# Gated linear attention and two feed-forward layers: attention products split into 64-column tiles

## The chip, the cores and the metric

One Trainium2 chip, one core. The metric is the device time of one execution in microseconds, the median of several runs. TensorE (PE in the profile) does the matrix products, VectorE (DVE), ScalarE (ACT) and GpSimd (POOL) the rest, and SyncE (SP) issues the DMAs. The stationary operand of a product is loaded into the array by an instruction of its own, LDWEIGHTS (PEld in the profile); the MATMUL then streams the other operand through. The array has 128 rows (the contraction) and 128 columns (the stationary operand's columns, which become the output's partitions).

## The reference

Three layers. First a gated linear attention, for 4 batch entries and 8 heads of 48, over 768 positions:

```python
f = 1.0 / (1.0 + np.exp(-f_logit))
for t in range(S):
    state = f[:, :, t, :, None] * state + np.einsum('bhd,bhe->bhde', k[:, :, t], v[:, :, t])
    y[:, :, t] = np.einsum('bhd,bhde->bhe', q[:, :, t], state)
```

The outputs of the 8 heads side by side are 3,072 rows of 384. Then a normalised, gated layer of width 1,536, `(silu(xn @ w_gate) * (xn @ w_val)) @ w_out` with `xn = x / rms * rms_g`, and a layer of width 2,048, `g(x @ w_in) @ w_out` with a piecewise quadratic `g`. All data are fp32.

## The kernel before, in words

The 768 positions are cut into 6 chunks of C = 128. A **unit** u is one chunk of one batch entry: 24 units, chunk n = u // 4, batch entry b = u % 4. `attention` (L382) does one unit for all 8 heads, which are taken in NP = 4 pairs p. A pair of heads lies on partitions 0 to 47 and 64 to 111 (HP = 64; PD = 112 rows in use), so that one product serves both heads or each head has one half of the rows. Inside a chunk the recurrence becomes products, with q and k scaled by running products of the gates (scans on VectorE, L419 to L430):

- `turned` (L433, products on L435) transposes k, 4 products.
- `scores` (L442, products on L446): for each p and each head i, the 128 x 128 matrix of k against q; k of 48 rows and 128 columns is stationary, q streams 128 columns. 8 products, alternating between rows 0 to 47 and 64 to 111. VectorE multiplies the two score tiles by the causal mask (L449), tile W (or sg).
- `update` (L454, products on L456): for each p, transposed k (112 columns) stationary, v of both heads (96 columns) streams. The result has the two 48 x 48 blocks wanted, one for each head, and two that belong to no head. 4 products. VectorE adds the wanted blocks to the state (L481, or L486 in the first chunk), so that the blocks that no head owns stay zero. The units of the last chunk leave this out.
- `read` (L466): for each p, q against the state of the pair (L471; 128 stationary columns, 96 streamed; not in the first chunk, where the state is zero), then for each head the masked scores against v (L473; 128 stationary columns, 48 streamed), all accumulated in tile y. 4 x (1 + 2) = 12 products.

Each of these fp32 products stands as two LDWEIGHTS and two MATMUL records in the trace. Then the row norm (L489 to L495), a transposition (`xpose`, L500, on L502), and a split into a high and a low part, xh and xl (L511, L513), for the next layer.

The feed-forward products are done in three parts of a narrower fp32 (`mm3`, L517, on L519 to L521): high by high, low by high, high by low, each 128 x 128 stationary and 512 streamed (the 4 batch entries of one chunk), one record each. For each chunk j, 12 steps of the first layer (gate, value, output) make 324 such products; after the 6 chunks the second layer follows, 6 x 16 steps. Weights are loaded and split into two parts once (`weights`, L349; L365 to L376 on ScalarE, VectorE and GpSimd), those of the first layer before and during the first chunk.

The order on every engine is made by a planner (`Plan`, L50) before the program runs: `add` gives it each operation with its engine, a cost in ns, a due position and, for TensorE, the streamed columns; it simulates the engines and emits the operation that can start first, by due position where several can. The units of chunk j + 1 are due spread over the projections of chunk j. Units 0 to 3 come before the first projection; there the planner fills TensorE's idle time with products that nothing reads (`keep_clock`, L571, on L574). PSUM tiles are few: two "a" (transposed k, scores, update, transposition), two "h" (projections), three "o", one "y".

Of the kernel before, what the change touches and what calls it, by code (L numbers as in the profile page):

```python
# [16 lines left out]
B, H, S, D = 4, 8, 768, 48  # L17
C = 128
NCH = S // C
NU = NCH * B  # L20
NP = H // 2
HP = 64
PD = HP + D
VD = 2 * D
# [25 lines left out]
class Plan:  # L50
# [28 lines left out]
    def add(self, eng, cost, pos, fn, r=(), w=(), new=(), after=(), cols=0, at=0.0, table=None, lock=False):  # L79
        i = len(self.ops)  # L80
        deps = set(after)
        for key in r:
            deps.update(self.writer.get(key, ()))
        for key in w:
            deps.update(self.writer.get(key, ()))
            deps.update(self.readers.get(key, ()))
        for tag, key in new:
            if tag != "a" and tag in self.last:
                self.turn.setdefault(i, []).append(self.last[tag])
            self.last[tag] = i  # L90
            self.maker[key] = i
        for key in (*r, *w):
            base = key[0] if isinstance(key, tuple) else key
            if base in self.maker:
                deps.add(self.maker[base])
        for key in w:
            self.writer[key] = (i,)
            self.readers[key] = []
        for key in r:
            self.readers.setdefault(key, []).append(i)  # L100
        deps.discard(i)
        where = {eng: cost} if isinstance(eng, str) else {}
        if not where:
            for e, c in eng.items():
                if isinstance(c, tuple):
                    self.away[i, e] = c[1]
                    c = c[0]
                where[e] = c
        self.ops.append([where, None, pos, fn, deps, tuple(new), set(k for k in (*r, *w)), not isinstance(eng, str), cols, at, table, lock])
        return i  # L110
# [140 lines left out]
def dve(n, fast=False):  # L251
    return (65 + (n / 2 if fast else n)) / 0.96
# [6 lines left out]
def pool(n):  # L259
    return 250 + 2.0 * n  # L260
# [20 lines left out]
def gla_moe_moe2_kernel(ctx, tc, q, k, f, v, w_in, w_out, rms_g, w2, ident, cmask, hmask, out):  # L281
    nc = tc.nc
    pl = Plan()
    pl.engines = {"DVE": nc.vector, "Pool": nc.gpsimd, "ACT": nc.scalar}
    T = pl.T
    add = pl.add
# [38 lines left out]
    st = [const.tile([PD, NP, VD], F32, name=f"st{b}") for b in range(B)]  # L325
# [54 lines left out]
    updated = []  # L380

    def attention(u, due, g):  # L382
        n, b = divmod(u, B)
        last = u + B >= NU
        early = u < B
        fk, Fk, kk, qk, vk, yk, xk = (f"{nm}{u}" for nm in ("f", "F", "k", "q", "v", "y", "xn"))
        guest = early and u >= 2
        if guest:
            g0 = f"e{u}"
            kk, qk, vk, fk = ((g0, nm) for nm in ("k", "q", "v", "f"))  # L390
            fk = ("e4", "f" if u == 2 else "g")

        def at(x):
            return due + (x - 11) * g

        def v4(key):
            return T[key][0:PD].rearrange("p (a b) -> p a b", a=NP)
# [4 lines left out]
        def rows(h):  # L402
            return slice(h * HP, h * HP + D)
# [3 lines left out]
        if early or u % 2 == 0:  # L407
            keys = [fk] if early else [f"f{u}", f"f{u + 1}"]
            for o, key in enumerate(keys):
# [4 lines left out]
                w=keys, table="sigmoid")  # L414
# [6 lines left out]
            r=[fk, "floor"], w=[Fk], new=[("F", Fk)], lock=True)  # L421
# [4 lines left out]
            r=["back"], w=[fk], lock=True)  # L426
# [4 lines left out]
        ktk, tpk, uk = f"kT{u}", f"tp{u}", f"U{u}"  # L431
        if not last:
            def turned():  # L433
# [4 lines left out]
                r=[tpk], w=[ktk], new=[("kT", ktk)])  # L438
        aks, wks = [f"a{u}_{i}" for i in range(2)], [f"W{u}_{i}" for i in range(2)]
        tags = [("h", "sg") if early and i else ("a", "W") for i in range(2)]  # L440

        def scores():  # L442
            kt, qt = v4(kk), v4(qk)
            for p in range(NP):
                for i in range(2):
                    nc.tensor.matmul(T[aks[i]][:, p * C:(p + 1) * C], lhsT=kt[rows(i), p], rhs=qt[rows(i), p], start=True, stop=True)  # L446
        scored = add("PE", 4 * 222, at(2), scores, cols=1536, r=[kk, qk], w=aks, new=[(tags[i][0], aks[i]) for i in range(2)])
        for i in range(2):
            add("DVE", dve(4 * C), at(2 + i), lambda ak=aks[i], wk=wks[i]: nc.vector.tensor_tensor(  # L449
                T[wk].rearrange("p (a b) -> p a b", a=4), T[ak].rearrange("p (a b) -> p a b", a=4),  # L450
                cm.rearrange("p (o a) -> p o a", o=1).to_broadcast([C, 4, C]), op=ALU.mult),
                r=[aks[i], "cm"], w=[wks[i]], new=[(tags[i][1], wks[i])])
        if not last:
            def update():  # L454
                for p in range(NP):
                    nc.tensor.matmul(T[uk][0:PD, p * VD:(p + 1) * VD], lhsT=T[ktk][:, p * PD:(p + 1) * PD],  # L456
                                     rhs=T[vk][:, p * VD:(p + 1) * VD], start=True, stop=True)
            updated.append(add("PE", 4 * 196, at(5), update, cols=4 * 384, r=[ktk, vk], w=[uk], new=[("a", uk)], after=[scored]))

        def block(h):  # L460

            return st[b][rows(h), :, h * D:(h + 1) * D]
# [3 lines left out]
        def read():  # L466
            y, vt = T[yk], T[vk]
            for p in range(NP):
                c0 = p * VD
                if n:  # L470
                    nc.tensor.matmul(y[:, c0:c0 + VD], lhsT=v4(qk)[:, p], rhs=st[b][:, p], start=True, stop=False)  # L471
                for h in range(2):
                    nc.tensor.matmul(y[:, c0 + h * D:c0 + (h + 1) * D], lhsT=T[wks[h]][:, p * C:(p + 1) * C],  # L473
                                     rhs=vt[:, c0 + h * D:c0 + (h + 1) * D], start=(n == 0), stop=(n == 0 or h == 1))
        add("PE", 4 * (444 + (224 if n else 0)), at(6), read, cols=4 * (384 + (384 if n else 0)),
            r=[*wks, vk, qk, *(sks if n else [])], w=[yk], new=[(ytag, yk)])
        if not last:
            for h in range(2):
                uu = lambda h=h: T[uk][rows(h), 0:NP * VD].rearrange("p (a b) -> p a b", a=NP)[:, :, h * D:(h + 1) * D]
                if n:  # L480
                    add("DVE", dve(NP * D), at(8), lambda h=h, uu=uu: nc.vector.tensor_tensor(  # L481
                        block(h), block(h), uu(), op=ALU.add), r=[uk], w=[sks[h]])
                    add({"Pool": pool(NP * D), "DVE": dve(NP * D)}, 0, at(18), lambda eng, h=h: eng.tensor_tensor(
                        block(h), block(h), ends_of[rows(h)].to_broadcast([D, NP, D]), op=ALU.mult), r=[("fca", u)], w=[sks[h]], lock=True)
                else:
                    add("DVE", dve(NP * D), at(18), lambda h=h, uu=uu: nc.vector.tensor_tensor(  # L486
                        block(h), uu(), ends_of[rows(h)].to_broadcast([D, NP, D]), op=ALU.mult), r=[uk, ("fca", u), "zero"], w=[sks[h]])
# [4 lines left out]
            r=[ssk], w=[msk], new=[("ms", msk)])  # L492
        add("Pool", 520, at(8), lambda: nc.gpsimd.tensor_tensor(T[rik], T[msk], mhalf, op=ALU.pow),
            r=[msk, "halves"], w=[rik], new=[("ri", rik)])
# [14 lines left out]
        def tv():  # L509
            return T[tk][:, 0:DM].rearrange("p (a b) -> p a b", a=KD)  # L510
        add("ACT", act(DM, True), at(11), lambda: nc.scalar.copy(halves_of(xh), tv()),  # L511
            r=[tk], w=[(xh, o)], new=[("xh", xh)] if o == 0 else [])
        return add("DVE", dve(DM), at(11), lambda: nc.vector.tensor_tensor(  # L513
            halves_of(xl), tv(), halves_of(xh).bitcast(F32), op=ALU.subtract),
            r=[tk, (xh, o)], w=[(xl, o)], new=[("xl", xl)] if o == 0 else [])
# [73 lines left out]
    for u in range(B):  # L589
        attention(u, due0[u], 0.7)  # L590
# [9 lines left out]
    for j in range(NCH):  # L600
        step = SEG * (base[j + 1] - base[j]) / long
        if j + 1 < NCH:
            for o in range(B):
                done = attention(B * (j + 1) + o, base[j + 1] - 3.0 - (B - 1 - o) * (long + FILL) / B * 0.95, 2.0)
        oks = [f"o{e}_{j}" for e in range(KD)]
        xk = (f"xh{j}", f"xl{j}")
        for i in range(F1):
            p0 = base[j] + 3 * i * step
            gk, vk = f"hg{j}_{i}", f"hv{j}_{i}"
            sk = f"sg{j}_{i}"  # L610
            seg_in(gk, wk1[i][0], xk, range(B), p0)
            add("ACT", act(TB, True), p0 + step, lambda sk=sk, gk=gk: nc.scalar.activation(  # L612
                T[sk], T[gk], AF.Silu), r=[gk], w=[sk], new=[("sg", sk)], table="silu")
            seg_in(vk, wk1[i][1], xk, range(B), p0 + step)
            add("DVE", dve(TB), p0 + 2 * step, lambda sk=sk, vk=vk: nc.vector.tensor_tensor(  # L615
                T[sk], T[sk], T[vk], op=ALU.mult), r=[vk], w=[sk])
            phk, plk = split_p(sk, p0 + 2 * step)
            seg_out(oks, wk1[i][2], phk, plk, p0 + 5 * step, i == 0, i == F1 - 1)
        evac(oks, [x1d[j][:, e] for e in range(KD)], [("x1d", j, e) for e in range(KD)],
             base[j] + 3 * F1 * step + 3 * step, ["ev", "F", "ev"])  # L620
# [4 lines left out]
    for j in range(NCH):  # L625
        b0 = base2 + 2 * F2 * SEG * j
        xk = (f"xh2_{j}", f"xl2_{j}")
        for e, tg in enumerate(("f", "q", "f")):
            rk = f"x1r{j}_{e}"
            load(lambda rk=rk: T[rk][:, 0:TB], x1d[j][:, e], 128 * 2048, b0 - 44 + 4 * e, rk, [(tg, rk)],  # L630
                 r=[(("x1d", j, e), 0)], after=[done])
            add("ACT", act(512), b0 - 24 + 4 * e, lambda rk=rk, e=e, xk=xk: nc.scalar.copy(T[xk[0]][:, e], T[rk][:, 0:TB]),
                r=[rk], w=[(xk[0], 10 + e)], new=[("xh", xk[0])] if e == 0 else [])
            add("DVE", dve(512), b0 - 24 + 4 * e, lambda rk=rk, e=e, xk=xk: nc.vector.tensor_tensor(
                T[xk[1]][:, e], T[rk][:, 0:TB], T[xk[0]][:, e].bitcast(F32), op=ALU.subtract),
                r=[rk, (xk[0], 10 + e)], w=[(xk[1], 10 + e)], new=[("xl", xk[1])] if e == 0 else [], lock=True)
# [18 lines left out]
    def count():  # L655
# [5 lines left out]
        r=["mn", "hm"], w=["cnt"], new=[("a", "cnt")])  # L661
# [185 lines left out]
```

## Time and profile before

| | |
|---|---|
| median of 3 runs | 998.58 us (998.14 to 999.08) |
| the profiled execution's own time | 997.97 us |
| its span, from the first to the last instruction | 996.2 us |
| mean granted TensorE clock in it | 0.997 of full |
| busy: TensorE, VectorE, ScalarE, GpSimd | 983.0, 583.2, 357.3, 78.4 us |
| matmul records | 5064 |

How to read it: busy times are of one profiled execution. Matmuls overlap each other, and their ends are modelled; a record's duration is longer than its distance from the next one, so the cost of a group is read from the distance between starts. A busy share is a mean over stages with different limits; the table of stretches parts them.

### The profile page before, as it was taken

The numbers are of one execution on the slowest core, as the hardware profiler recorded it, in microseconds if no ns is written. First come the engines' busy times: TensorE is split into PE (matmuls) and PEld (weight loads), VectorE is DVE, ScalarE is ACT, GpSimd is POOL, SyncE is SP. The second block draws the span as 40 slices with busy tenths as digits, with TensorE's granted clock in tenths as the row PEclk, the third lists the DMA queues.
The fourth block names the chain that finished last, engine by engine and source line by source line (L and its number), as shares of the span: only waits on it lengthen the run. The fifth ranks groups of instructions, "written<-read, shape, count | busy, mean of one in ns | idle before, by whom it ended". The sixth has DMA issues, their size and how long they took to land.

```text
span 996.2 us, 12717 instructions
## 1 busy us (share of the span) xinstructions
PE 983.0 (99%) x5064; PEld 820.5 (82%) x5064; DVE 583.2 (59%) x886; ACT 357.3 (36%) x590; POOL 78.4 (8%) x82
## 2 busy tenths in 40 slices
PE   8999999999999999999999999999999999999997
PEld 7888888888888888888888888888888888888885
DVE  6998966335633563365336997555565555655544
ACT  3465623322432242223224555333343333333332
POOL 2404121001000110011000100000000000000000
PEclk9999999999999999999999999999999999999999
DMA  9971112101211121011005541010010010100001
GB/s 279 340 244 38 38 50 70 36 29 58 67 28 45 48 70 36 29 62 56 22 1 190 189 159 64 1 64 1 0 64 1 22 43 1 64 1 0 32 1 35
DMA packets 26500, 64.22 MB, mean 64 GB/s; under 512 B 3136, under 2 KB 6848, under 8 KB 26432
## 3 DMA queue, kind: packets, MB, share of 16 engines
q1 hardware_dynamic: 26432, 63.32, 19.8%
q8 instruction: 42, 0.69, 0.3%
q14 instruction: 26, 0.21, 0.1%
HBM read 53.87 MB, written 9.44 MB: 64 GB/s over the span
## 4 chain that ended last, share of the span: by engine, by line


## 5 line engine op out<-in xcount | busy, mean ns | idle before, releaser
L519 PE MATMUL h<-xh,w 128*128 128x512 f32 x720 | 284.2, 395 | 0.0
L521 PE MATMUL h<-xh,w 128*128 128x512 f32 x720 | 280.7, 390 | 0.0
L520 PE MATMUL h<-xl,w 128*128 128x512 f32 x720 | 280.2, 389 | 0.0
L519 PE MATMUL o<-ph,w 128*128 128x512 f32 x504 | 199.1, 395 | 0.0
L520 PE MATMUL o<-pl,w 128*128 128x512 f32 x504 | 196.6, 390 | 0.0
L521 PE MATMUL o<-ph,w 128*128 128x512 f32 x504 | 196.6, 390 | 0.0
L521 PEld LDWEIGHTS h<-xh,w 128*128 128x128 f32 x720 | 135.1, 188 | 28.8
L519 PEld LDWEIGHTS h<-xh,w 128*128 128x128 f32 x720 | 135.2, 188 | 27.9
L520 PEld LDWEIGHTS h<-xl,w 128*128 128x128 f32 x720 | 135.3, 188 | 27.1
L646 DVE SCALAR_TENSOR_TENSOR k<-sg,h 128x512 f32<-128x512 f32 x96 | 66.1, 688 | 97.8 <-ACT sg L644 97.2
L615 DVE TENSOR_TENSOR sg<-sg,h 128x512 f32<-128x512 f32 x72 | 49.2, 683 | 123.3 <-PE h L521 122.5
L520 PEld LDWEIGHTS o<-pl,w 128*128 128x128 f32 x504 | 94.7, 188 | 20.1 <-DVE pl L556 1.3
L519 PEld LDWEIGHTS o<-ph,w 128*128 128x128 f32 x504 | 94.7, 188 | 19.9
L521 PEld LDWEIGHTS o<-ph,w 128*128 128x128 f32 x504 | 94.6, 188 | 19.8
L555 ACT CAST ph<-k 128x512 fp32r<-128x512 f32 x96 | 59.5, 619 | 132.3 <-DVE k L648 132.3
L644 ACT ACTIVATE sg<-h,halves 128x512 f32<-128x512 f32 x96 | 66.1, 688 | 113.4 <-PE h L521 113.4
L556 DVE TENSOR_TENSOR pl<-k,ph 128x512 fp32r<-128x512 f32 x96 | 66.5, 692 | 64.6 <-ACT ph L555 64.6
L612 ACT ACTIVATE sg<-h 128x512 f32<-128x512 f32 x72 | 43.0, 597 | 116.6 <-PE h L521 116.5
L555 ACT CAST ph<-sg 128x512 fp32r<-128x512 f32 x72 | 44.6, 620 | 109.7 <-DVE sg L615 109.7
L648 DVE SCALAR_TENSOR_TENSOR k<-sg,k 128x512 f32<-128x512 f32 x96 | 66.5, 692 | 3.0
L556 DVE TENSOR_TENSOR pl<-sg,ph 128x512 fp32r<-128x512 f32 x72 | 51.9, 721 | 21.3 <-ACT ph L555 21.0
L473 PE MATMUL y<-v,W 128*128 128x48 f32 x328 | 47.1, 265 | 0.0
(114 smaller groups left out, 851.2 us busy)
## 6 DMA issues: line engine op xcount, KB each, us to landing
w<-in_w SPq DMA_DIRECT2D x16, 768.0 KB, 4.5
w<-in_w_in SPq DMA_DIRECT2D x12, 768.0 KB, 11.8
k<-in_k SPq DMA_DIRECT2D x22, 256.0 KB, 2.8
f<-in_f SPq DMA_DIRECT2D x22, 226.6 KB, 2.7
q<-in_q SPq DMA_DIRECT2D x22, 224.0 KB, 2.8
w<-in_w_out SPq DMA_DIRECT2D x6, 768.0 KB, 11.9
v<-in_v SPq DMA_DIRECT2D x22, 192.0 KB, 2.8
x1d<-ev SPq DMA_DIRECT2D x12, 256.0 KB, 2.0
```

Of the source, the lines that this page charges most:

```text
L473: nc.tensor.matmul(y[:, c0 + h * D:c0 + (h + 1) * D], lhsT=T[wks[h]][:, p * C:(p + 1) * C], rhs=vt[:, c0 + h * D:c0 + (h + 1) * D], start= ...
L519: nc.tensor.matmul(o, lhsT=wh, rhs=xh, start=start, stop=False)
L520: nc.tensor.matmul(o, lhsT=wh, rhs=xl, start=False, stop=False)
L521: nc.tensor.matmul(o, lhsT=wl, rhs=xh, start=False, stop=stop)
L555: add("ACT", act(TB), pos, lambda: nc.scalar.copy(T[phk], T[pk]), r=[pk], w=[phk], new=[("ph", phk)])
L556: add("DVE", dve(TB), pos, lambda: nc.vector.tensor_tensor(T[plk], T[pk], T[phk].bitcast(F32), op=ALU.subtract), r=[pk, phk], w=[plk], new ...
L612: add("ACT", act(TB, True), p0 + step, lambda sk=sk, gk=gk: nc.scalar.activation(T[sk], T[gk], AF.Silu), r=[gk], w=[sk], new=[("sg", sk)], ...
L615: add("DVE", dve(TB), p0 + 2 * step, lambda sk=sk, vk=vk: nc.vector.tensor_tensor(T[sk], T[sk], T[vk], op=ALU.mult), r=[vk], w=[sk])
L644: add("ACT", act(512, True, 1), p0 + SEG, lambda ak=ak, hk=hk: nc.scalar.activation(T[ak], T[hk], AF.Relu, bias=half, scale=0.5), r=[hk, " ...
L646: add("DVE", dve(512), p0 + SEG, lambda ak=ak, gk=gk, hk=hk: nc.vector.scalar_tensor_tensor(T[gk], T[ak], 1.0, T[hk], op0=ALU.min, op1=ALU ...
L648: add("DVE", dve(512), p0 + SEG, lambda ak=ak, gk=gk: nc.vector.scalar_tensor_tensor(T[gk], T[ak], 1.0, T[gk], op0=ALU.min, op1=ALU.mult), ...
```

## The change

Three of the four groups of products are cut in two. In `scores` and `read` the stationary operand's 128 columns become two products of 64, whose outputs are partitions 0 to 63 and 64 to 127 of the same tile; each half streams what the whole did. In `update` each pair's product becomes two, one for each head: 48 stationary columns, 48 streamed, the output on partitions 0 to 47 and 64 to 111; the blocks that belong to no head are not computed, and the result lies 48 instead of 96 columns apart. The costs and columns that the planner is told are changed with them.

```diff
         def scores():
             kt, qt = v4(kk), v4(qk)
             for p in range(NP):
-                for i in range(2):
-                    nc.tensor.matmul(T[aks[i]][:, p * C:(p + 1) * C], lhsT=kt[rows(i), p], rhs=qt[rows(i), p], start=True, stop=True)
-        scored = add("PE", 4 * 222, at(2), scores, cols=1536, r=[kk, qk], w=aks, new=[(tags[i][0], aks[i]) for i in range(2)])
+                for x in range(2):
+                    for i in range(2):
+                        nc.tensor.matmul(T[aks[i]][x * HP:(x + 1) * HP, p * C:(p + 1) * C], lhsT=kt[rows(i), p, x * HP:(x + 1) * HP],
+                                         rhs=qt[rows(i), p], start=True, stop=True)
+        scored = add("PE", 600, at(2), scores, cols=1200, r=[kk, qk], w=aks, new=[(tags[i][0], aks[i]) for i in range(2)])
...
             def update():
                 for p in range(NP):
-                    nc.tensor.matmul(T[uk][0:PD, p * VD:(p + 1) * VD], lhsT=T[ktk][:, p * PD:(p + 1) * PD],
-                                     rhs=T[vk][:, p * VD:(p + 1) * VD], start=True, stop=True)
-            updated.append(add("PE", 4 * 196, at(5), update, cols=4 * 384, r=[ktk, vk], w=[uk], new=[("a", uk)], after=[scored]))
+                    for h in range(2):
+                        nc.tensor.matmul(T[uk][rows(h), p * D:(p + 1) * D], lhsT=T[ktk][:, p * PD + h * HP:p * PD + h * HP + D],
+                                         rhs=T[vk][:, p * VD + h * D:p * VD + (h + 1) * D], start=True, stop=True)
+            updated.append(add("PE", 550, at(5), update, cols=1200, r=[ktk, vk], w=[uk], new=[("a", uk)], after=[scored]))
...
             for p in range(NP):
                 c0 = p * VD
-                if n:
-                    nc.tensor.matmul(y[:, c0:c0 + VD], lhsT=v4(qk)[:, p], rhs=st[b][:, p], start=True, stop=False)
+                for x in range(2 if n else 0):
+                    nc.tensor.matmul(y[x * HP:(x + 1) * HP, c0:c0 + VD], lhsT=v4(qk)[:, p, x * HP:(x + 1) * HP], rhs=st[b][:, p],
+                                     start=True, stop=False)
                 for h in range(2):
-                    nc.tensor.matmul(y[:, c0 + h * D:c0 + (h + 1) * D], lhsT=T[wks[h]][:, p * C:(p + 1) * C],
-                                     rhs=vt[:, c0 + h * D:c0 + (h + 1) * D], start=(n == 0), stop=(n == 0 or h == 1))
-        add("PE", 4 * (444 + (224 if n else 0)), at(6), read, cols=4 * (384 + (384 if n else 0)),
+                    for x in range(2):
+                        nc.tensor.matmul(y[x * HP:(x + 1) * HP, c0 + h * D:c0 + (h + 1) * D],
+                                         lhsT=T[wks[h]][:, p * C + x * HP:p * C + (x + 1) * HP],
+                                         rhs=vt[:, c0 + h * D:c0 + (h + 1) * D], start=(n == 0), stop=(n == 0 or h == 1))
+        add("PE", 4 * (230 + (170 if n else 0)) + 150, at(6), read, cols=4 * (384 + (384 if n else 0)),
             r=[*wks, vk, qk, *(sks if n else [])], w=[yk], new=[(ytag, yk)])
         if not last:
             for h in range(2):
-                uu = lambda h=h: T[uk][rows(h), 0:NP * VD].rearrange("p (a b) -> p a b", a=NP)[:, :, h * D:(h + 1) * D]
+                uu = lambda h=h: T[uk][rows(h), 0:NP * D].rearrange("p (a b) -> p a b", a=NP)
```

## Rows read from the trace of the kernel before

**Rows 1.** The page: busy times, the slices of TensorE, the costliest groups (two of six).

```profile
PE 983.0 (99%) x5064; PEld 820.5 (82%) x5064; DVE 583.2 (59%) x886; ACT 357.3 (36%) x590; POOL 78.4 (8%) x82
...
PE   8999999999999999999999999999999999999997
...
L519 PE MATMUL h<-xh,w 128*128 128x512 f32 x720 | 284.2, 395 | 0.0
...
L519 PE MATMUL o<-ph,w 128*128 128x512 f32 x504 | 199.1, 395 | 0.0
```

**Rows 2.** Timeline of TensorE among projections; start us, us, engine, line, what.

```profile
301.21 0.39 PE L519 MATMUL h<-xh,w 128*128 128x512 f32 x1
...
303.25 0.39 PE L519 MATMUL h<-xh,w 128*128 128x512 f32 x1
```

**Rows 3.** Table of stretches: length; PE, PEld, DVE, ACT, POOL busy; PEclk; DMA share; GB/s.

```profile
25.00:45.18 20.18, 19.79 (x194) 17.66 (x195) 18.86 (x33) 8.32 (x21) 10.65 (x8) 1.00 1.03 335
45.18:135.88 90.70, 90.50 (x509) 76.33 (x507) 83.46 (x119) 53.25 (x80) 22.77 (x19) 1.00 0.34 111
142.00:239.00 97.00, 96.63 (x547) 81.44 (x546) 45.69 (x76) 28.38 (x52) 8.68 (x11) 1.00 0.16 47
520.00:990.00 470.00, 469.08 (x2068) 386.88 (x2066) 283.93 (x412) 178.18 (x274) 2.57 (x1) 1.00 0.14 48
```

**Rows 4.** TensorE's waits, longest total first; total us, times, longest.

```profile
PE a L456 <- ACT kT L437: 2.0, 1, 2.0
```

**Rows 5.** TensorE's groups by line, 45.1 to 519 us: the read's.

```profile
L473 PE MATMUL y<-v,W 128*128 128x48 f32 x320 | 45.6, 265 | 0.0
L471 PE MATMUL y<-st,q 112*128 112x96 f32 x160 | 33.1, 288 | 0.0
```

**Rows 6.** Timeline of TensorE around one unit's scores.

```profile
309.68 0.39 PE L520 MATMUL h<-xl,w 128*128 128x512 f32 x1
309.91 0.39 PE L521 MATMUL h<-xh,w 128*128 128x512 f32 x1
310.23 1.16 PE L446 MATMUL a<-q,k 48*128 48x128 f32 x16
311.32 0.50 PE L519 MATMUL h<-xh,w 128*128 128x512 f32 x1
```

**Rows 7.** Timeline of TensorE: scores of a unit with score tiles a and h.

```profile
34.04 0.27 PE L446 MATMUL a<-w 48*128 48x128 f32 x1
34.05 0.27 PE L446 MATMUL h<-w 48*128 48x128 f32 x1
34.15 0.27 PE L446 MATMUL a<-w 48*128 48x128 f32 x1
```

**Rows 8.** Timeline of TensorE: an update, its read at once behind it.

```profile
317.58 0.93 PE L456 MATMUL a<-v,kT 128*112 128x96 f32 x8
318.34 0.39 PE L471 MATMUL y<-st,q 112*128 112x96 f32 x2
...
318.97 0.43 PE L471 MATMUL y<-st,q 112*128 112x96 f32 x2
...
319.64 0.43 PE L471 MATMUL y<-st,q 112*128 112x96 f32 x2
...
320.97 0.48 PE L519 MATMUL h<-xh,w 128*128 128x512 f32 x1
```

**Rows 9.** Timeline of TensorE's weight loads among projections.

```profile
309.68 0.19 PEld L521 LDWEIGHTS h<-xh,w 128*128 128x128 f32 x1
```

**Rows 10.** Timeline of TensorE: an update with projections behind it.

```profile
390.38 0.93 PE L456 MATMUL a<-v,kT 128*112 128x96 f32 x8
391.09 0.48 PE L519 MATMUL h<-xh,w 128*128 128x512 f32 x1
```

**Rows 11.** Timeline of TensorE before the first projection.

```profile
41.21 2.47 PE L574 MATMUL o<-spin 128*128 128x256 bf16 x21
...
43.84 1.58 PE L574 MATMUL o<-spin 128*128 128x256 bf16 x13
```

## The prediction

> **What bounds the kernel now.** I began with the page's busy shares and its slices: TensorE is busy 99% of the span, and in every slice but the first and the last [rows 1]. Matmul ends are modelled, so I checked this on start times. In the projections one 512-column matmul follows another every 2.04/9 = 0.227 us [rows 2], and the 3 x (720 + 504) = 3,672 of them [rows 1] make 834 us of the 996.2 us span. The table of stretches, read next, says what else is near its limit: TensorE is full in each of them. VectorE is busy 83.46 of 90.70 us while the first chunk's projections run, and only 45.69 of 97.00 us in a later chunk; from 520 us on, where no attention is left, the change can touch nothing [rows 3]. The list of TensorE's waits is short: the longest totals 2.0 us [rows 4]. So from 45 us to 518 us each microsecond taken off TensorE's own stream is a microsecond off the end, if VectorE keeps up.
>
> What TensorE spends on attention there: scores, update, and the read's two groups, the state's on L471 and the values' on L473. Each fp32 product makes two records: 20 units x 4 p x 2 heads are 160 products, and 320 records [rows 5]. For one unit (one batch entry, one chunk) the timeline gives:
>
> Scores, 16 records, take 311.32 - 310.23 = 1.09 us [rows 6]. In a unit whose two score tiles have different names (a and h) the records can be told apart: the two heads' records, on rows 0 to 47 and 64 to 111, start within 0.01 us of each other, and such a pair starts every 0.111 us [rows 7]. Two row halves thus run side by side. Eight pairs are 0.89 us; the other 0.20 us, and 0.09 us ahead of the block (0.32 us since the last projection record where 0.227 is usual), are what going into and out of this split costs: 0.29 us.
>
> The update takes 0.76 us (8 records of 112 stationary columns, 0.095 each) and the read 2.63 us (24 records) [rows 8]. One p of the read is 6 records in 0.67 us, 0.111 each, though two of them stream 96 columns and four only 48. What they share is a load of 128 stationary columns. So the load sets the pace: 0.111/128 = 0.87 ns a column, and the update's 0.095/112 = 0.85 agrees.
>
> **The change, part by part.** Every product is split into twice as many with 64 stationary columns (48 in the update), on alternate column halves. No row shows a column split. The question is whether the two halves' loads run side by side, as row halves do [rows 7], or in turn. Side by side, a pair costs 64 x 0.87 = 0.056 us where one record cost 0.111; in turn it costs 0.111 and nothing is won. These are the two ends. I take the first, as the row split is the nearest row: same loads, same instruction, a different half.
>
> The Trainium skill ("TensorE: Matmul & The Clock Gate", Part 3, What overlaps and what doesn't) has a rule against this: weight loads overlap with running matmuls only where the row group differs, and column halves share theirs. By it the loads go in turn (second rival). As a general rule this trace contradicts it: the load for L521 starts at 309.68, with the L520 matmul of the same 128 rows [rows 9, 6].
>
> Scores: 8 groups of four records instead of 8 pairs, 8 x 0.056 = 0.45, and the same 0.20 around them: 0.65 against 1.09, saves 0.44. The split by rows was there already, so no new entry is paid. x20 units = 8.8 us.
>
> Update: 8 pairs of 48 columns, 8 x 48 x 0.87 ns = 0.34 against 0.76, saves 0.42. The last chunk has none: x16 = 6.7 us. That the diagonal blocks alone are made also halves the streamed columns, worth nothing by itself, since the load sets the pace.
>
> Read: 24 pairs, 24 x 0.056 = 1.34 against 2.63, saves 1.29; x20 = 25.8 us.
>
> New entries and exits: update and read had no split around them, and now each run of them pays the 0.29 us of the scores. In 11 of the 16 units with an update the read follows it at once, in 5 projections stand between [rows 8, 10]. With the four units that only read that is 20 + 5 = 25 runs, 7.3 us to pay. The bounds are 20 runs at no new cost, and 40 runs at 0.29 = 11.6. The order is written by a planner that now gets other costs, so the count may change.
>
> Sum for the 20 units: 8.8 + 6.7 + 25.8 - 7.3 = 34.0 us.
>
> VectorE as cover: its work is not changed by the edit (the update's result is read with a denser stride, same elements). The first chunk holds 4 of the 20 units, each good for 0.44 + 0.42 + 1.29 less 0.36 (1.25 runs), 1.8 us; by 4 x 1.8 = 7.2 us it would shrink from 90.7 to 83.5 us, against VectorE's 83.46 [rows 3]. VectorE has gaps and would not be full to the last tenth. GpSimd, 22.77 of 90.70, can take some of the work that is allowed on either. Loss between 0 and 7.2; I take 2.5. Later chunks have half of VectorE free.
>
> Units 0 to 3, before 45 us: fillers surround their products (34 of them from 41.21 to 45.18), and VectorE is busy 18.86 of 20.18 us from 25.00 on [rows 3, 11]. Shorter scores and reads mostly become more fillers. A gain can come only where VectorE waited for scores, at most about 0.44 + 4 x 4 x 0.056 = 1.3 us for one unit's chain; the bounds are -1 (a worse order) and +1.3, I take 0.5.
>
> Instructions: 1,088 more records and as many loads, no DMA added or moved, no new wait, so nothing on another engine or queue stands behind a later instruction.
>
> Total: 34.0 - 2.5 + 0.5 = 32.0 us. The profiled execution took 997.97 us, 1.8 us more than its span and 0.6 us less than the median of 998.58, within the spread of the runs; taken from the median, **966.6 us**. Best ends (no new entries, no VectorE loss, head +1.3) give 998.6 - 42.6 = 956; the worst ends of the same case (40 runs, loss 7.2, head -1) 998.6 - (41.3 - 11.6 - 7.2 - 1.0) = 977.
>
> **Rivals.** *Loads side by side, streams in turn.* If the halves share the path of the streamed operand, a pair lasts at least two streams, at 0.227/512 = 0.44 ns a column. Scores: 2 x 128 columns = 0.114, no gain. State products: 2 x 96 = 0.085 instead of 0.056. The rest stays load-bound. Read saves 24 x 0.111 - 8 x 0.085 - 16 x 0.056 = 1.09, update 0.42: 20 x 1.09 + 16 x 0.42 - 7.3 = 21.2. The first chunk then shrinks by some 4 us and VectorE fills 96% of it, for which I take off 1.4: 978.8 us. For it: no row shows two streams into different columns of the same rows at once. Against: two row halves take their streams together [rows 7]. Chance 0.13.
>
> *Loads in turn* (slower). A pair costs 2 x 0.056 = 0.111, as one record does now: scores and read gain nothing, the update 0.76 - 16 x 48 x 0.87 ns = 0.09. The entries stay: 20 + 5 runs x 0.29 = 7.3, less 16 x 0.09 = 1.5: 5.8 us more, 1004.4. What the products save falls in a line from 41.3 us at 0.056 a pair to 1.5 at 0.111, so it drops under the 7.3 of the entries once a pair takes over 0.103. Against it stand the row halves. Chance 0.08.
>
> *The sequencer's pace* (slower). Side by side asks for a record every 0.014 us in the scores and 0.028 us in the read. The fastest sustained in this trace is 16 records in 0.89 us, 0.056 each [rows 7]. If that were the floor: scores 32 x 0.056 = 1.79 + 0.20, 0.90 more; update 16 x 0.056 = 0.90, 0.14 more; read 48 x 0.056 = 2.69, 0.06 more. 20 x 0.96 + 16 x 0.14 + 7.3 = 28.7 more: 1027 us. Against: the two matmuls of a pair start inside 0.01 us, so the engine takes them quicker when they are there. "TensorE: Matmul & The Clock Gate" of the Trainium skill (Part 1) gives about 62 ns a matmul where the sequencer decodes in software; the 0.056 of rows 7 is below that, which speaks for the hardware path. Chance 0.06.
>
> *VectorE becomes the bound in the first chunk entirely*: 7.2 lost instead of 2.5, 971 us; this is inside the forecast's own range.
>
> **How the numbers follow.** Forecast 0.68, streams in turn 0.13, loads in turn 0.08, the sequencer 0.06; 0.05 for mixtures, such as halves that overlap only in part with all the entries paid, 0.03 of it within 0.2% (2 us, about what a measurement of this kernel can tell from no change) and 0.02 faster. Faster 0.68 + 0.13 + 0.02 = 0.83, same 0.03, slower 0.14. The range runs from the best ends, 956, to 984, the streams in turn with the worst first chunk and order; it holds nearly all of the first two cases, 0.80.
>
> **What would show each step.** Right: in the timeline the scores' block lasts about 0.65 us, update and read adjacent about 0.34 + 1.34 + 0.29 = 2.0 us instead of 3.39, the two halves' loads start within some 0.01 us of each other, and a later chunk takes 97.0 - 4 x 1.8 = about 90 us. Streams in turn: scores stay at 1.09, state pairs stand 0.085 apart. Loads in turn: pairs 0.111 apart, read 2.6 us and more. Sequencer: an even 0.056 per record whatever its size. VectorE: a first chunk over 88 us with idle on TensorE ended by VectorE. A lower granted clock than 1.00 after 45 us [rows 3], the 2.4 GHz level now, would upset every term; no row points to it, as the row split of the scores doesn't lower it.

## The result, and the profile after

The changed kernel takes 982.01 us (median; 981.18 to 983.35, 4 runs) against 998.83 us for the kernel before: a ratio of 0.9827 (95% interval in brackets here and below) [0.9803, 0.9851], 16.8 us less. The forecast was 966.6 us, 32.0 us less. The time lies inside the range of 956 to 984, the direction is the forecast one, and a little over half of the gain came. The profiled execution took 981.18 us, with a span of 979.3 us against 996.2.

The page of the changed kernel first, busy times and TensorE's slices: still full from the second slice to the last but one, as in [rows 1], with more records.

```profile
PE 964.0 (98%) x6210; PEld 788.9 (81%) x6210; DVE 580.4 (59%) x882; ACT 358.0 (37%) x590; POOL 88.8 (9%) x86
...
PE   8999999999999999999999999999999999999997
```

Its table of stretches (columns as in [rows 3]), cut where the projections of the first chunk begin and where those of the second and a later one begin:

```profile
25.00:46.10 21.10, 20.84 (x319) 17.57 (x317) 18.98 (x32) 8.25 (x18) 8.97 (x8) 1.00 1.03 352
46.10:138.25 92.15, 91.67 (x704) 72.97 (x701) 81.89 (x121) 53.30 (x81) 25.92 (x19) 1.00 0.30 103
231.52:324.79 93.27, 92.05 (x738) 74.97 (x736) 45.48 (x75) 28.47 (x52) 11.19 (x12) 1.00 0.16 49
```

From one chunk's first projection to the next one's, a later chunk went from 96.81 to 93.27 us and the first from 94.90 to 92.15. VectorE is busy 81.89 of 92.15 us there, 89%: it didn't become the bound. The first projection starts at 46.10 instead of 45.18.

Timeline of TensorE around a unit's scores, to be held against [rows 6]:

```profile
302.24 0.39 PE L527 MATMUL h<-xh,w 128*128 128x512 f32 x1
302.56 1.10 PE L447 MATMUL a<-q,k 48*64 48x128 f32 x32
303.59 0.50 PE L525 MATMUL h<-xh,w 128*128 128x512 f32 x1
```

The block lasts 1.03 us, not the forecast 0.65. A unit with two named score tiles shows the groups of four [rows 7]:

```profile
25.72 0.27 PE L447 MATMUL a<-w 48*64 48x128 f32 x1
25.72 0.27 PE L447 MATMUL h<-w 48*64 48x128 f32 x1
25.73 0.27 PE L447 MATMUL a<-w 48*64 48x128 f32 x1
25.74 0.27 PE L447 MATMUL h<-w 48*64 48x128 f32 x1
25.83 0.27 PE L447 MATMUL a<-w 48*64 48x128 f32 x1
```

All four start within 0.02 us of each other (by the starts of single records so do their four loads), and such a group comes every 0.109 us. So the halves do run at once; what is left of the time is not the load of 64 columns.

Timeline of TensorE over an update and its read, against [rows 8]:

```profile
309.66 0.39 PE L527 MATMUL h<-xh,w 128*128 128x512 f32 x1
309.98 0.56 PE L459 MATMUL a<-v,kT 128*48 128x48 f32 x16
310.37 0.35 PE L474 MATMUL y<-st,q 112*64 112x96 f32 x4
...
310.77 0.35 PE L474 MATMUL y<-st,q 112*64 112x96 f32 x4
...
312.07 0.50 PE L525 MATMUL h<-xh,w 128*128 128x512 f32 x1
```

The update takes 0.39 us (0.76 before), the read 1.70 (2.63 before), one p of the read 310.77 - 310.37 = 0.40 us (0.67 before). By the starts of single records an update's pair comes every 0.045 us and a value pair every 0.058, as forecast; a state pair costs about 0.085, (0.40 - 4 x 0.058)/2, and not 0.056.

Last, one of the scores' blocks that wait. The transposition just ahead of it holds one of the two tiles a, and the scores need both. The bracket says how long TensorE sat idle and which operation ended that: VectorE's subtraction that makes xl, the last reader of the transposition's tile:

```profile
257.16 0.49 PE L508 MATMUL a<-idt,xn 128*128 128x128 f32 x3
257.58 0.43 PE L447 MATMUL a<-q,k 48*64 48x128 f32 x2
258.81 1.10 PE L447 MATMUL a<-q,k 48*64 48x128 f32 x30 [0.80 <-DVE xl L519]
```

This block lasts 2.26 us, 1.22 over the usual. Summed over the starts of blocks between the first projection and the last transposition, the two traces give this ledger (us saved):

| | forecast | trace |
|---|---|---|
| scores, blocks without waits | 8.8 | 1.1 |
| update, 8 pairs a unit | 6.7 | 6.3 |
| read, 24 pairs a unit | 25.8 | 20.2 |
| entries and exits of the split | -7.3 | -6.2 |
| TensorE's waits (forecast: lost to VectorE) | -2.5 | -4.7 |
| before the first projection | 0.5 | -0.9 |
| rest (transpositions, the end) | 0 | 1.1 |
| sum | 32.0 | 16.9 |

Two terms carry the miss: scores, 7.7 us, and read, 5.6 us. Of the 4.7 us of waits 3.1 lie in the scores' blocks, the other 1.6 in projections of the first chunk. The forecast counted 20 scores' blocks; 19 lie behind the first projection (0.44 us of its 8.8).

### The profile page after: what moved, and what is told of

It is laid out like the page before. It is cut to its first block, busy times and chain, and to the rows that moved or that the text cites. A ratio compares the mean times of both kernels' runs of the same rounds, so it can differ in the third digit from the quotient of the medians.

```text
span 979.3 us, 15022 instructions
## 1 busy us (share of the span) xinstructions
PE 964.0 (98%) x6210; PEld 788.9 (81%) x6210; DVE 580.4 (59%) x882; ACT 358.0 (37%) x590; POOL 88.8 (9%) x86
## 4 chain that ended last, share of the span: by engine, by line
## 5 line engine op out<-in xcount | busy, mean ns | idle before, releaser
L451 DVE TENSOR_TENSOR W<-a,cm 128x512 f32<-128x512 f32 x44 | 28.8, 683 | 20.5 <-PE a L447 20.5
```

## The experiments

Each one is a change of the changed kernel unless it says otherwise. The kernel before ran beside them at 998.4 to 999.1 us (medians).

**The scores' split undone.** The first theory was the prediction's second case: loads side by side, streams in turn.

```diff
-                for x in range(2):
-                    for i in range(2):
-                        nc.tensor.matmul(T[aks[i]][x * HP:(x + 1) * HP, p * C:(p + 1) * C], lhsT=kt[rows(i), p, x * HP:(x + 1) * HP],
-                                         rhs=qt[rows(i), p], start=True, stop=True)
+                for i in range(2):
+                    nc.tensor.matmul(T[aks[i]][:, p * C:(p + 1) * C], lhsT=kt[rows(i), p], rhs=qt[rows(i), p], start=True, stop=True)
...
```

> The scores' split undone (8 whole products, told cost as before), update and read split. Theory (loads of the two column halves go side by side, their streams in turn): the scores' block is 1.09 us instead of 1.03, and the projections behind it lose 0.12 us less, so 20 units come out 0 to 2 us faster than the changed kernel: 980 to 982 us. Rival (the split of the scores does save what its loads save, and something else costs the missing 15 us): 9 us slower, about 991 us.

982.11 us, ratio 0.9825 [0.98, 0.9849]: the same as with the split. A block without waits is 1.09 us; the projections' overhead, their time over 0.227 us each, falls from 14.1 to 12.1 us in all. Only 0.4 us of these 2.0 lie directly behind the scores' blocks (0.16 us a block split, 0.14 whole), so the 0.12 us a block that the expectation names is not there. The split of the scores is worth nothing. The rival falls.

**Shorter streams for half of the scores.**

```diff
-                        nc.tensor.matmul(T[aks[i]][x * HP:(x + 1) * HP, p * C:(p + 1) * C], lhsT=kt[rows(i), p, x * HP:(x + 1) * HP],
-                                         rhs=qt[rows(i), p], start=True, stop=True)
+                        nc.tensor.matmul(T[aks[i]][x * HP:(x + 1) * HP, p * C + x * HP:(p + 1) * C], lhsT=kt[rows(i), p, x * HP:(x + 1) * HP],
+                                         rhs=qt[rows(i), p, x * HP:C], start=True, stop=True)
...
```

> Scores split as in the changed kernel, but the upper half of the key rows streams only queries 64 to 127 (the rest is masked to zero anyway; the zeros are written by GpSimd, the mask is two VectorE operations). Loads unchanged, streams 128 + 64 columns for 128 + 128. Theory (streams in turn): a group of four records takes 192 x 0.44 = 0.085 us instead of 0.109, the block 0.85 instead of 1.03, about 4 us faster: 978 us, less what VectorE's extra operation costs in the first chunk. Rival (a sequencer that starts a record every 0.027 us): the group stays at 0.109 and the time at 982 us.

990.18 us, ratio 0.9911 [0.9887, 0.9936]. Of the 8 us over the changed kernel 6.7 arise before the first projection, which starts at 52.78 us; that the additions of GpSimd and VectorE delay it is likely, not shown. The block itself hardly moved:

```profile
312.09 1.09 PE L447 MATMUL a<-q,k 48*64 48x128 f32 x32
313.11 0.50 PE L531 MATMUL h<-xh,w 128*128 128x512 f32 x1
```

1.02 us, not 0.85. With 64 of 256 streamed columns gone a group takes as long as before: the theory of streams in turn falls here. The sequencer's pace is still standing, and so is a third reading: side by side, but slow.

**The old costs for the planner, all products split.**

```diff
-        scored = add("PE", 600, at(2), scores, cols=1200, r=[kk, qk], w=aks, new=[(tags[i][0], aks[i]) for i in range(2)])
+        scored = add("PE", 4 * 222, at(2), scores, cols=1536, r=[kk, qk], w=aks, new=[(tags[i][0], aks[i]) for i in range(2)])
...
-            updated.append(add("PE", 550, at(5), update, cols=1200, r=[ktk, vk], w=[uk], new=[("a", uk)], after=[scored]))
+            updated.append(add("PE", 4 * 196, at(5), update, cols=4 * 384, r=[ktk, vk], w=[uk], new=[("a", uk)], after=[scored]))
...
-        add("PE", 4 * (230 + (170 if n else 0)) + 150, at(6), read, cols=4 * (384 + (384 if n else 0)),
+        add("PE", 4 * (444 + (224 if n else 0)), at(6), read, cols=4 * (384 + (384 if n else 0)),
```

> All products split as in the changed kernel, but the planner is told the costs and columns of the kernel before. Theory (some 4 to 5 us of the changed kernel are stalls and a later first projection, which come from the order): with the order planned on the old costs the stalls fall back to about 3.8 us: 977 to 979 us. Rival (the order does not matter): 982 us.

981.32 us, ratio 0.9823 [0.9789, 0.9856]: no difference that can be measured from 982.01. A later chunk takes 93.06 us (93.27 with the new costs), and the scores' waits only moved: two of the three blocks that waited 1.22 us are gone, five that wait 0.3 to 0.4 are new. The rival is right.

**The state for one half alone.**

```diff
-                for x in range(2 if n else 0):
+                for x in range(1 if n else 0):
```

(The values' products of the other half then each start their own sum.)

> The state's share of the read is made for output rows 0 to 63 alone; rows 64 to 127 go without it. Theory (streams in turn, a single half streams at full rate): a record of 96 streamed columns stands alone at its load's 0.058 us, one p of the read takes 0.35 us instead of 0.40, 20 units 4 us less: 978 us. Rival (a split stream runs at half rate also when it is alone): the record takes 0.085 us, one p stays at 0.40, 982 us.

982.44 us, ratio 0.9827 [0.9803, 0.9851]. The timeline shows one p of the read from 312.08 to 312.48:

```profile
312.08 0.26 PE L474 MATMUL y<-st,q 112*64 112x96 f32 x1
312.08 0.26 PE L478 MATMUL y<-v,W 128*64 128x48 f32 x1
312.18 0.25 PE L474 MATMUL y<-st,q 112*64 112x96 f32 x1
312.18 0.46 PE L478 MATMUL y<-v,W 128*64 128x48 f32 x7
312.48 0.26 PE L474 MATMUL y<-st,q 112*64 112x96 f32 x1
```

Still 0.40 us. The record of 96 columns takes its 0.1 us although the other half streams only 48 beside it: taken in turn at 0.44 ns a column, 96 + 48 would be 0.064. It also speaks against the sequencer's pace, as 8 of 48 records are gone. The rival of this run is right, but it was put too narrowly: the slow stream need not belong to the split. The next two runs part that.

**The kernel before, with a wide stream and no column split.**

```diff
-                    nc.tensor.matmul(T[uk][0:PD, p * VD:(p + 1) * VD], lhsT=T[ktk][:, p * PD:(p + 1) * PD],
-                                     rhs=T[vk][:, p * VD:(p + 1) * VD], start=True, stop=True)
+                    w = 2 * VD if p + 1 < NP else VD
+                    nc.tensor.matmul(T[uk][0:PD, p * VD:p * VD + w], lhsT=T[ktk][:, p * PD:(p + 1) * PD],
+                                     rhs=T[vk][:, p * VD:p * VD + w], start=True, stop=True)
```

> The kernel before, nothing split by columns; in the update three of the four p stream 192 columns of v instead of 96 (what lies beyond the pair's 96 is written over by the next p's product, so nothing is lost). The load of 112 columns, 0.097 us, stays. New theory (an fp32 record streams a column in 0.83 ns, half the rate of the projections' narrower fp32, whether split or not, and the column halves stream side by side): a wide record takes 192 x 0.83 = 0.160 us instead of 0.097, 6 of them 0.38 us a unit, 16 units 6 us slower: 1005 us. Rival (fp32 streams at 0.44 ns a column as long as the array is whole; the column split halves the rate): 192 x 0.44 = 0.085 us hides under the load, the update stays at 0.77 us and the time at 999 us.

1006.1 us, ratio 1.0067 [1.0041, 1.0092]: 0.7% slower, clear of noise. The update went from 0.77 us [rows 8] to 1.16:

```profile
323.69 1.32 PE L457 MATMUL a<-v,kT 128*112 128x192 f32 x8
324.85 0.39 PE L472 MATMUL y<-st,q 112*128 112x96 f32 x2
```

By the starts of blocks it is 1.153 against 0.768, 0.064 us for each of the six wide records; 0.097 + 0.064 = 0.161 us for 192 columns, 0.84 ns a column, in the whole array. So an fp32 record streams at about half the rate of the projections' narrower fp32, 0.44 ns, and no split is needed for that. The split records fit about the same price: a state pair of 96 columns at 0.085, a group of four of 128 at 0.109, the wide record of 192 at 0.161 us.

**A split stream that is not fp32.**

```diff
-        nc.tensor.matmul(T["spare"][:, 0:256], lhsT=z[:, 0:128], rhs=z[:, 0:256], start=True, stop=True)
+        nc.tensor.matmul(T["spare"][0:HP, 0:256], lhsT=z[:, 0:HP], rhs=z[:, 0:256], start=True, stop=True)
```

> The changed kernel; the filler products before the first projection (bf16, 256 streamed columns, nothing reads them) are made with 64 stationary columns on one column half instead of 128. New theory (the slow stream belongs to fp32): a filler stays at 0.109 us where the granted clock is 1.00. Rival (the column split halves the rate of any stream): 0.213 us at a granted clock of 1.00. Time within 2 us of 982 by either, unless the granted clock in the first 45 us changes.

983.8 us (one run). The last fillers before the first projection, first line, and in the same place of the kernel before, 13 whole ones, 1.58 us [rows 11]:

```profile
46.63 1.61 PE L580 MATMUL o<-spin 128*64 128x256 bf16 x13
```

A split filler comes every 0.109 us at a granted clock of 1.00, like a whole one. A product on one column half is not slowed by being on a half, and the rival falls; two halves at once in bf16 were not tried.

**Scores of the diagonal blocks alone.** Each half streams its own 64 queries; queries 64 to 127 with keys 0 to 63 are left out.

```diff
-                        nc.tensor.matmul(T[aks[i]][x * HP:(x + 1) * HP, p * C:(p + 1) * C], lhsT=kt[rows(i), p, x * HP:(x + 1) * HP],
-                                         rhs=qt[rows(i), p], start=True, stop=True)
+                        nc.tensor.matmul(T[aks[i]][x * HP:(x + 1) * HP, p * C + x * HP:p * C + (x + 1) * HP], lhsT=kt[rows(i), p, x * HP:(x + 1) * HP],
+                                         rhs=qt[rows(i), p, x * HP:(x + 1) * HP], start=True, stop=True)
...
```

> Scores split as in the changed kernel, but each half streams only its own 64 queries; the scores of queries 64 to 127 with keys 0 to 63 are left out (zeros in their place, written by GpSimd; the mask is two VectorE operations). New theory (halves side by side, 0.83 ns a column): a group of four records takes its load's or its stream's 0.053 us and 0.005, 0.058 instead of 0.109, the block about 0.63 us instead of 1.03. Rival (a sequencer that starts one record every 0.027 us): the group stays at 0.109, the block at 1.02. GpSimd's and VectorE's additions before 45 us can make the whole slower by either, as in the run with the triangle.

987.22 us (one run; the first projection starts at 51.20). The block:

```profile
310.58 0.70 PE L447 MATMUL a<-q,k 48*64 48x64 f32 x32
311.21 0.50 PE L532 MATMUL h<-xh,w 128*128 128x512 f32 x1
```

0.63 us for 32 records, as the new theory says: 0.65 was also the forecast for the whole scores, which took the load alone as the pace. By the starts of single records a group of four comes every 0.058 us, a record every 0.015 on the mean, with loads as before and half of the streamed columns. So neither the sequencer nor the loads set the 0.109 us of the changed kernel's groups; the streams do.

**The waits.** First, told costs that were measured (with whole scores):

```diff
-        scored = add("PE", 4 * 222, at(2), scores, cols=1536, r=[kk, qk], w=aks, new=[(tags[i][0], aks[i]) for i in range(2)])
+        scored = add("PE", 1300, at(2), scores, cols=1536, r=[kk, qk], w=aks, new=[(tags[i][0], aks[i]) for i in range(2)])
```

(The update's 550 became 500 and the read's 150 became 210.)

> Scores whole, update and read split, and the planner told what the blocks were measured to cost with the entry, the exit and the slower projections behind them: scores 1300, update 500, read 1810 instead of 888, 550 and 1750. Theory (a part of the stalls comes of costs told too low): the scores' blocks over 1.2 us (8 of 19, 8.1 us over the usual in the run with whole scores) become fewer, 2 to 4 us faster than that run: 978 to 980 us. Rival (the stalls are the latency from the transposition or its copy to the scores, which no cost of TensorE's changes): 982 us.

983.54 us, ratio 0.9844 [0.9817, 0.9871]; the scores' blocks wait 10.3 us in all (7.8 with whole scores and the old told cost). The theory falls: what the planner is told does not take these waits away. Then another tile for the transposition:

```diff
-        add("PE", 330, at(11), xpose, cols=768, r=[xk, "idt"], w=[tk], new=[("a", tk)])
+        add("PE", 330, at(11), xpose, cols=768, r=[xk, "idt"], w=[tk], new=[("a" if early else "y", tk)])
```

> The changed kernel; from the second chunk's units on the transposition writes the PSUM tile y, which its own unit has just set free, instead of one of the two tiles a. Theory (a part of the missing time is the wait of the scores, which need both tiles a, for the copy of a transposition just ahead of them; in the changed kernel three scores' blocks wait 1.22 us each for it): these waits go, 3 to 4 us faster: 978 to 979 us. Rival (the wait only moves to the next thing that is late, the scaled k or the copy of kT): 982 us.

978.17 us, ratio 0.9797 [0.978, 0.9813]. The place shown above, in this run:

```profile
256.13 0.49 PE L508 MATMUL y<-idt,xn 128*128 128x128 f32 x3
256.55 1.10 PE L447 MATMUL a<-q,k 48*64 48x128 f32 x32
```

No wait inside the scores; all three blocks of 2.26 us are gone, three of 1.88 are left, and a later chunk takes 92.15 us. The shared tile was the cause of these three. With the transposed k in y too (`new=[("h" if early else "y", tpk)]`):

> As in the run before, and the transposed k goes to tile y as well, so that the scores and the update have the two tiles a for themselves. Theory (as above; the three scores' blocks that wait 0.85 us for the copy of kT are the same wait for a tile a): another 2.5 us, 975 to 977 us. Rival (tile y is now shared by four uses in a fixed order, and the transposition of k waits for the unit before it): no faster than the run before, or slower.

978.52 us, ratio 0.98 [0.9783, 0.9818]. A later chunk takes 91.15 us, 1.0 less, but the first takes 95.50 instead of 92.15, with a wait of 2.7 us of the scores for VectorE's state. Both sides were right in part. The same with whole scores:

> As in the run before, with the scores' products whole as they were in the kernel before (told cost as before). Theory (the split of the scores wins nothing, since 128 streamed fp32 columns take as long as the load of 128 columns): the same as the run before within 1.5 us. Rival (the split of scores pays once nothing waits around it): 1.5 to 3 us slower.

976.87 us, ratio 0.9785 [0.9769, 0.9801], 1.65 us less than the run before, a little outside the 1.5 expected; but a later chunk takes 91.31 us against 91.15, so the split of the scores is worth 0.04 us a unit: nothing. The difference in time between the two runs lies in the first chunk (94.41) and before it. Last, the transposed k in y only from the third chunk's units on, against the changed kernel and beside the edit of the transposition above:

```diff
-            add("PE", 440, at(1), turned, cols=4 * 196, r=[kk, "idt"], w=[tpk], new=[("h" if early else "a", tpk)], after=updated[-1:])
+            add("PE", 440, at(1), turned, cols=4 * 196, r=[kk, "idt"], w=[tpk], new=[("h" if early else "a" if u < 2 * B else "y", tpk)], after=updated[-1:])
```

> The changed kernel with transposition in tile y from the second chunk's units on, and the transposed k there only from the third chunk's units on, so that the first stretch of projections keeps the order of the run with the transposition alone in y (92.14 us where the run with both in y took 95.50) and the later ones take 91.15 instead of 92.15. Theory: 3.3 us less than the run with both in y in the first stretch, 4 x 1.0 less than the other in the later four but one: 974 to 976 us. Rival (the wait that the first stretch showed comes back in a later one, since the tiles a are short wherever the transposed k first moves): 977 to 979 us.

976.31 us (974.71 to 976.47), ratio 0.9766 [0.9744, 0.9789]: the lowest median here, 5.7 us under the changed kernel, though not to be told from the 976.87 us of the run before. It lies just above the 974 to 976 us of the theory. The stretches are 92.16 and 91.15 us, as expected; in the profiled execution the first projection starts at 47.67 us, 1.6 later than in the run with the transposition alone in y (46.12), by the same order of instructions up to there. All 19 scores' blocks take 1.03 us, and the three longest of TensorE's waits total 3.7 us; none is for the low half xl that frees a transposition's tile, and the third is the update's for the copy of the transposed k:

```profile
PE h L435 <- DVE k L429: 1.9, 1, 1.9
PE o L580 <- DVE spin L573: 1.1, 1, 1.1
PE a L459 <- ACT kT L437: 0.7, 1, 0.7
```

## Why the prediction was right or wrong

The direction was right, and the time lies in the range, but this is in part luck: the bounds of the forecast's own case were 956 to 977 us, and 982.01 lies beyond them. The range reached to 984 to hold the streams in turn, a mechanism that the runs refute.

**Loads side by side**: right. Four quarters of the array start together, value pairs stand 0.058 apart (forecast 0.056), update pairs 0.045 (0.042). The Trainium skill's rule, "TensorE: Matmul & The Clock Gate", Part 3, by which loads overlap running matmuls only in another row group, would have made them go in turn; the trace disagrees, with two column halves of the same rows 0.01 us apart, their loads as well as their matmuls, in the groups of four shown above.

**"So the load sets the pace"**: this is the step that failed. It was read from the read, where 48 or 96 streamed columns hid under a load of 0.111 us, and carried over to what is left when the load is halved. At the 0.84 ns a column of the wide update an fp32 record streams 128 columns in some 0.107 us (an estimate), about as long as 128 columns take to load (0.111 a record in the read). In the kernel before, the two limits of the scores lay on top of each other, and nothing in [rows 6] or [rows 7] tells them apart. Halving the load left the stream: a group of four takes 0.109 instead of 0.056 (7.7 us of the miss), a state pair 0.085 instead of 0.056 (8 x 0.029 x 20 units = 4.6 us of the read's 5.6; what the other 1.0 is was not taken apart). The price of a streamed column that the prediction used, 0.44 ns, came from the projections, which run in the narrower fp32; it appeared only in the first rival, where it was too low by a factor of about two as well. "FP8 and Floating Point Precision" of the Trainium skill (TensorE Precision Notes) gives four passes for true fp32; with two records for a product that is two passes a record, and the 0.84 ns of the wide update agrees.

**Streams in turn**, the first rival, had come out at 978.8 us, nearest to the result of all the cases, and with the right signs: scores gain nothing, state pairs 0.085. Its mechanism is still refuted. Two streams in turn at 0.44 ns and two at once at 0.84 ns take nearly the same time, as long as both halves stream equally many columns; the runs with the triangle and with one half of the state broke that tie. Loads in turn and the sequencer's pace are refuted by the same traces, the latter by 32 records in 0.63 us.

**Entries and exits**: right in size, 6.2 us for 26 runs against 7.3 for 25.

**VectorE as cover**: VectorE did not become the bound of the first chunk, at 89% busy. The prediction's stretch for it ends at 135.88 us, 4.2 before the next chunk's first projection at 140.08; over the whole stretch VectorE had 85.40 of 94.90 us. The sign named for VectorE, a first chunk over 88 us with idle on TensorE ended by VectorE, is met only in the letter (92.15 us, 0.3 us of idle): the chunk is long because a unit saves 0.9 us (3.54 / 4 in a later chunk), not 1.8. TensorE lost 4.7 us more to waits than before. The 3.1 us in the scores' blocks are for the second tile a; the 1.6 in the first chunk's projections end, by the trace, with VectorE's pl and sg and with a piece of a weight that GpSimd makes, so VectorE did cost something there. Three of TensorE's waits in the changed kernel (total us, times, longest):

```profile
PE a L447 <- DVE xl L519: 2.6, 4, 0.8
PE a L447 <- ACT kT L437: 1.5, 4, 0.4
PE o L526 <- DVE pl L562: 0.3, 1, 0.3
```

In the kernel before the first of these was 0.7 us, once. The prediction had the list of waits [rows 4] but took the order as it was; the new order put a transposition directly ahead of the scores in three places instead of one.

**Before the first projection**: 0.9 us lost instead of 0.5 won. The granted clock (below) does not account for it: in the first 25 us it was 0.93 on the mean in the kernel before and 1.00 in the changed one, and the run with the transposition in y, with the changed kernel's order up to there, has 0.93 and starts at 46.12 as well. The cause stays open.

## What to carry to other kernels

Before halving one limit, price the next one in the same number format: here the load of 128 columns and the stream of 128 fp32 columns take about equally long, and only the products that stream fewer columns than they load gained from narrower tiles. Two explanations that give the same sum are told apart by making the two sides unequal, not by the time of the whole. A small loss around a faster block is worth a look at which buffer it shares: one PSUM tile moved gave a quarter of what the whole change gave.

## What the runs showed of the hardware that was not expected

The granted clock before the first projection differs between executions of one order of instructions. In the changed kernel's profile it was 1.00 of the 2.4 GHz level on the mean of the first 25 us; with one half of the state left out, where the first 45 us are the same program, it was 0.86, so some 7 of the 25 us, 2 x 0.14 x 25, passed at the 1.2 GHz level. The stretch in the changed kernel, and in the other run:

```profile
0.00:25.00 25.00, 21.16 (x276) 16.91 (x277) 18.27 (x31) 9.09 (x18) 8.94 (x14) 1.00 0.95 279
```

```profile
0.00:25.00 25.00, 21.36 (x260) 16.82 (x262) 15.96 (x28) 8.06 (x16) 9.72 (x14) 0.86 0.96 284
```

In the other run TensorE had stood idle for 2.6 us, until 11.05, for the k that VectorE scales; the clock was 0.50, the 1.2 GHz level, from 11 to 17 us, with TensorE busy again, and 1.00 from 18 on. The kernel before has the same picture: 2.0 us idle, for kT [rows 4], from 12 us on, and 0.50 from 14 to 17 us. In the changed kernel's profile the longest two waits of TensorE lasted 1.5 and 1.3 us, and the clock stayed at 1.00. What decides it is not shown. The first projection starts at 46.10 us in the one and at 47.61 in the other. Two more runs have the same order up to there: with the transposition alone in y it starts at 46.12, at a mean clock of 0.93, and with the transposed k moved later as well at 47.67, at 0.86. So about 1.5 us of the spread between runs arises there.
